# Scaled keys turned on VectorE in place of TensorE from chunk 12 on, in a fused linear-attention and maximum-of-three MLP kernel

## The chip, the cores and the metric

The kernel runs on one core of a Trainium2 chip. The metric is the device time of one execution in microseconds (us); less is better. A core has the engines TensorE (PE in the rows; PEld is its weight load), VectorE (DVE), ScalarE (ACT), GpSimd (POOL) and SyncE (SP), each with a queue of its own that it works through in order, and 16 DMA engines.

## The reference

A recurrent attention over 4 batches, 8 heads, 768 steps and 48 channels per head, and then an MLP whose hidden layer is the maximum of three products:

```python
for t in range(S):
    kt, vt, rt, wt = (k[:, :, t], v[:, :, t], r[:, :, t], w[:, :, t])
    cur = np.einsum('bhd,bhe->bhde', u[None] * kt, vt)
    y[:, :, t] = np.einsum('bhd,bhde->bhe', rt, state + cur)
    state = wt[:, :, :, None] * state + np.einsum('bhd,bhe->bhde', kt, vt)
...
h = np.maximum(np.maximum(x @ w1, x @ w2), x @ w3)
return (h @ w_out).astype(np.float32)
```

Here x is y laid out as 3072 tokens of 384 channels; the hidden layer has 768 channels. All inputs are float32.

## The kernel before

The sequence is cut into 6 chunks of 128 steps for each of the 4 batches, which makes 24 chunks k = 0 to 23 (the batch is k modulo 4, the place in the sequence k divided by 4). The attention of four chunks yields 512 tokens, a *half* in the program's words, and the MLP works on one half at a time: 18 groups of matmuls *up* (3 matrices x 6 blocks of the hidden layer; line 167), then 72 matmuls *down* (4 blocks of tokens x 6 blocks of the hidden layer x 3 terms; line 201). Apart from a part of the first half, each product is made of terms with a high and a low part of the operands (x_hi, x_lo, h_hi, h_lo), made by `split` (line 132 on ScalarE, line 133 on VectorE). `take_up` empties the PSUM tile of an up group: ScalarE copies the first of three (line 150), VectorE takes the maximum with the second and third (line 152).

A chunk of attention is a set of steps, each of one letter. Those that matter here:

- `b`, `p`, `q`, `f`, `r` (prep_scan_b to prep_rk): VectorE makes running products of the decay w forwards and backwards (scans at lines 399 and 414) and scales r and k in place in the loaded tile `tin` (line 423). The scaled keys, `kp`, lie with the channel in the partition: 112 partitions (two heads of 48, at 0 and at 64, with a gap of 16), 4 pairs of heads, 128 steps.
- `T` (transposes, line 492): turns `kp` so that the step lies in the partition: `kn`, 128 partitions, 4 pairs, 112 channels. TensorE does it by four transposes against `ident` (line 497) into a PSUM tile of the pool ps_m (four buffers, shared with the up and down groups and with `pu`), and ScalarE copies it out (line 499). Chunks 0 to 19 have this step; the last four pass no state on.
- `U` (to_state, line 518): TensorE multiplies `kn` with the values v into `pu`, the chunk's addition to the state; `S` (line 529) adds it on VectorE; `Z` (line 533) applies the decay.
- `X` (scores, line 477), `M` (take: a masked copy on VectorE, line 483, and a copy on ScalarE, line 486), `R` (from_state, line 508), `V` and `Y` (values, values_more, line 547): these make the chunk's output y in PSUM. Between V and Y stands a ScalarE copy of four columns of y, `touch` (line 553); Y's first matmul waits for it. `E` (result, line 565) copies y to x.
- `n` loads the next `tin` into one of three buffers, `tbuf[k % 3]`; `d`, `e` make the diagonal term, with GpSimd (lines 437, 438, 457).

The order of the work is written out by hand. Up to the end of the second half's MLP it is the string PARTS. After that six *units* for each k from 12 on are taken from the string ORD, and about one unit follows each MLP group; the number behind a letter is added to the chunk:

```python
ORD = "R0 V0 X1 Y0 U0 E0 b2 p2 d2 q2 | f2 n3 | S0 r2 Z2 c2 | e2 M1 | T1 | |"
```

So T for the next chunk comes in the fifth unit, and U uses its result in the first unit of the next round. Beside this runs `check_w` every third group: VectorE looks at a weight block (line 363), ScalarE squares and sums the result (line 365), and ScalarE's queue issues the load of the next block (line 368). ScalarE also empties the down groups (line 205), whose results SyncE's queue stores (line 688).

Of the kernel before, what the change touches and what calls it, by code (L numbers as in the profile page):

```python
# [29 lines left out]
F32 = mybir.dt.float32  # L30
# [11 lines left out]
B, H, S, D = 4, 8, 768, 48  # L42
DM, FF = 384, 768
NP = 4
C = 128
NCH = S // C
# [4 lines left out]
RK = -(-WU // 128) * 128  # L51
TU = RK + 2 * NP * C
# [40 lines left out]
PIECES = dict(a=(0, 1), b=(1, 2), c=(2, 4), d=(0, 2), e=(0, 4))  # L93
FIX = [*range(3 * FR, 3 * FT), *range(3 * FT + FR, NW), *range(3 * FR), *range(3 * FT, 3 * FT + FR)]
CS = 8
LATE = 2
LINE = 128
BIT = 16
# [4 lines left out]
def lines(n):  # L103

    return -(-n // LINE) * LINE
# [3 lines left out]
def kernel(ctx: ExitStack, tc, tin, nat, u_flat, u_pair, v_t, w_flat, out, ytr):  # L109
    nc = tc.nc  # L110
# [109 lines left out]
    with ExitStack() as fast:  # L220
# [6 lines left out]
        kn_p = pool("kn", 2)  # L227
# [9 lines left out]
        NB = 3  # L237
# [14 lines left out]
        def load(k):  # L252
            c, b = divmod(k, B)
            t = tbuf[k % NB]
            for cols in (slice(0, WU), slice(RK, TU)):
                if k == 0:
                    nc.sync.dma_start(out=t[0:64, cols], in_=tin[b, c, 0:64, cols])
                    nc.scalar.dma_start(out=t[64:112, cols], in_=tin[b, c, 64:112, cols])
                else:
                    nc.sync.dma_start(out=t[0:112, cols], in_=tin[b, c, :, cols])  # L260

        warm = cst.tile([128, 128], BF16, name="warm")
        nc.gpsimd.memset(warm[:, :], 0.0)
# [129 lines left out]
        prep = {}  # L393
# [23 lines left out]
        def prep_rk(k):  # L417

            t = tbuf[k % NB]
            both = t[:, RK:TU].rearrange("p (s a b) -> p s a b", s=2, a=NP)  # L420
            by = prep[k]["gf"][:, 0:2 * (WC + 2)].rearrange("p (s n) -> p s n", s=2)[:, :, 0:NP * WS]
            by = by.rearrange("p s (a b) -> p s a b", a=NP)[:, :, :, 0:C]
            nc.vector.tensor_tensor(out=both[0:112], in0=both[0:112], in1=by[0:112], op=ALU.mult)  # L423
            prep[k].update(rp=both[:, 0], kp=both[:, 1])

        def prep_check(k):
            flat = prep[k]["gf"][0:112, 0:2 * WC]
# [64 lines left out]
        def transposes(k):  # L492
            if goes_on(k):
                p = prep[k]
                pt = ps_m.tile([128, HT], F32, name="psm")
                for pr in range(NP):
                    nc.tensor.transpose(pt[:, pr * 112:pr * 112 + 112], p["kp"][0:112, pr, :], ident[0:112, 0:112])  # L497
                p["kn"] = kn = kn_p.tile([128, lines(NP * 112)], F32, name="kn")[:, 0:NP * 112].rearrange("p (a b) -> p a b", a=NP)
                nc.scalar.copy(out=kn[:, :, :].rearrange("p a b -> p (a b)"), in_=pt[:, 0:NP * 112])

        def from_state(k):
            p = prep.setdefault(k, {})
# [55 lines left out]
        def result(k):  # L558
# [11 lines left out]
            for lo in (0, 64) if due else ():  # L570
                for j in range(KT):
# [4 lines left out]
                     b=prep_scan_b, p=prep_floor, q=prep_inv, f=prep_scan_f, r=prep_rk, c=prep_check, d=prep_diag1, e=prep_diag2)  # L576
# [170 lines left out]
    with tc.If(rv != 0), ExitStack() as slow:  # L747
# [9 lines left out]
        with tc.For_i(0, B) as b:  # L757
            for pr in range(NP):
# [8 lines left out]
                for hh in range(2):  # L767
                    rows = slice(64 * hh, 64 * hh + 48)
# [90 lines left out]
def _layout(r, k, v, w, u, moe_w1, moe_w2, moe_w3, moe_w_out):  # L859

    def heads(a):
        return a.reshape(B, NP, 2, NCH, C, D).transpose(0, 3, 2, 5, 1, 4)

    tin = np.zeros((B, NCH, 112, TU), np.float32)
    tin[:, :, 48:64, :WC] = 1.0
    tin[:, :, :, :WC:WS] = 0.0
    for half in range(2):
        rows = tin[:, :, 64 * half:64 * half + D]
        rows[..., :NP * WS].reshape(B, NCH, D, NP, WS)[..., 1:] = heads(w)[:, :, half]
        rows[..., RK:RK + NP * C] = heads(r)[:, :, half].reshape(B, NCH, D, NP * C)  # L870
        rows[..., RK + NP * C:TU] = heads(k)[:, :, half].reshape(B, NCH, D, NP * C)
        rows[..., WC + half:WU:2] = u.reshape(NP, 2, D)[:, half].T

    def natural(a):
        return a.reshape(B, H, NCH, C, D).transpose(0, 2, 3, 1, 4).reshape(B, NCH, C, H * D)

    nv, turned = natural(v), lambda a: np.roll(a[..., H * D // 2:], HC, axis=2)
    parts = [nv, turned(nv)]
    for a in (natural(k), natural(r)):
        a = np.concatenate([a[..., 0:H * D // 2], turned(a)], axis=3)  # L880
        parts.append(a.reshape(B, NCH, C, NP, 2, D).swapaxes(3, 4).reshape(B, NCH, C, H * D))
    nat = np.concatenate(parts, axis=3)
    row = np.empty((KT, 128), np.int64)
    head = lambda j, par: 4 * (j % 2) + 2 * par + j // 2
    for j in range(KT):
        for par in range(2):
            row[j, 64 * par:64 * par + 48] = head(j, par) * D + np.arange(48)
            row[j, 64 * par + 48:64 * par + 64] = head(KT, par) * D + 16 * j + np.arange(16)
    ws = np.stack([moe_w1, moe_w2, moe_w3])
    w_in = ws[:, row.reshape(-1), :].reshape(3, KT, 128, FT, 128).transpose(3, 0, 2, 1, 4).reshape(3 * FT, 128, PC)  # L890
    w_all = np.concatenate([w_in, moe_w_out.reshape(FT, 128, DM)])
    if w_all.dtype == np.float64:
        w_all = np.append(w_all.reshape(-1), np.zeros(1)).view(np.int64)
    return {
        "tin": tin, "nat": nat, "u_flat": u.reshape(NP, 2, D).swapaxes(0, 1).reshape(H * D), "u_pair": u.reshape(NP, 2, D, 1),
        "v_t": v.transpose(0, 1, 3, 2), "w_all": w_all,
    }
# [18 lines left out]
```

## Time and profile before

| | |
|---|---|
| median of 3 runs | 414.88 us (414.78 to 415.26) |
| the profiled execution's own time | 414.63 us |
| its span, first to last instruction | 412.2 us |
| PE busy | 398.8 us (97%) |
| DVE busy | 266.1 us (65%) |
| ACT busy | 175.0 us (42%) |
| POOL busy | 83.9 us (20%) |
| granted TensorE clock, mean | 0.998 |

All times in rows are counted from the start of the span. The busy time of an engine counts each moment once, while the durations of its instructions overlap: the next one starts before the last has ended. The distance from start to start therefore tells more of a price than the duration. In the rows an operation is written as tile written <- tiles read, with partitions x elements; "x4" at the end of a row of the timeline says that four instructions are merged in it. What stands in brackets is the idle time of the engine just before, and what ended it.

### The profile page before, as it was taken

Reading aid. Unit: us, or ns where it says so; the run is one execution under the profiler, and the core shown is the slowest. Engines: PE = TensorE matmul, PEld = TensorE weight load, DVE = VectorE, ACT = ScalarE, POOL = GpSimd, SP = SyncE. Lnnn points to the kernel's source line nnn. Section 1 sums busy time; section 2 is a strip of 40 time slices with the busy share of each in tenths; the row PEclk is TensorE's granted clock in tenths of the full one; section 3 lists DMA queues with packets and bytes.
Section 4 is the critical chain, followed back from the end, with each engine's and each line's share of the span. In section 5 each row is a group of like instructions: output and inputs, shape, how many; then the busy total and the mean of one; then the engine's idle time right before and its main releaser. Section 6 shows DMA issues by size and latency. Waiting matters only on the chain.

```text
span 412.2 us, 9386 instructions
## 1 busy us (share of the span) xinstructions
PE 398.8 (97%) x3852; PEld 328.9 (80%) x3852; DVE 266.1 (65%) x446; ACT 175.0 (42%) x401; POOL 83.9 (20%) x92
## 2 busy tenths in 40 slices
PE   8898999899999999999999999999999999999994
PEld 3566877687788888988889988888978888988894
DVE  6998999997859777447568467658558623233320
ACT  1466667654543253514524534434534432411210
POOL 4240142404026141123303113203113100000000
PEclk9999999999999999999999999999999999999999
DMA  8948895902442150482643582533592121200001
GB/s 215 326 153 257 266 289 197 271 3 55 151 153 78 53 180 14 132 264 61 195 142 119 157 297 74 175 112 131 152 310 83 38 78 59 78 1 2 2 21 64
DMA packets 23844, 55.69 MB, mean 135 GB/s; under 512 B 3280, under 2 KB 6672, under 8 KB 23792
## 3 DMA queue, kind: packets, MB, share of 16 engines
q1 hardware_dynamic: 20160, 45.56, 36.1%
q10 hardware_dynamic: 3632, 9.44, 7.2%
q8 instruction: 32, 0.52, 0.5%
q14 instruction: 20, 0.16, 0.1%
HBM read 49.10 MB, written 4.72 MB: 131 GB/s over the span
## 4 chain that ended last, share of the span: by engine, by line
PE 83%; DVE 8%; DMA 3%; issue 2%; ACT 1%; SPq 1%; DVEq 0%; ACTq 0%
PE psm L167 53%; PE psm L201 15%; PE y L547 3%; DMA tin<-in_tin_dram 3%; PE grams L477 3%; PE y L508 3%; PE psm L518 2%; DVE gf L414 2%; PE grams L201 2%; PE psm L497 1%; DVE gf L399 1%; DVE tin L423 1%; DVE kr L434 1%; DVE w L342 1%; SPq L573 1%
## 5 line engine op out<-in xcount | busy, mean ns | idle before, releaser
L167 PE MATMUL psm<-x_hi,w 128*128 128x512 f32 x576 | 185.3, 395 | 0.0
L167 PEld LDWEIGHTS psm<-x_hi,w 128*128 128x128 f32 x576 | 108.1, 188 | 23.1 <-issue 0.2
L167 PE MATMUL psm<-x_lo,w 128*128 128x512 f32 x288 | 112.2, 390 | 0.0
L152 DVE TENSOR_TENSOR m<-psm,m 128x512 f32<-128x512 f32 x64 | 44.0, 688 | 70.3 <-PE psm L167 65.4
L457 POOL TENSOR_SCALAR_AFFINE_SELECT a<-sums 64x512 f32<-64x512 f32 x48 | 44.1, 919 | 207.2 <-DVE sums L453 117.6
L201 PE MATMUL psm<-w,h_hi 128*128 128x384 f32 x264 | 70.1, 362 | 0.0
L167 PEld LDWEIGHTS psm<-x_lo,w 128*128 128x128 f32 x288 | 54.1, 188 | 10.6
L201 PEld LDWEIGHTS psm<-w,h_hi 128*128 128x128 f32 x264 | 47.7, 188 | 4.9
L132 ACT CAST h_hi<-m 128x512 fp32r<-128x512 f32 x32 | 19.7, 620 | 52.2 <-DVE m L152 52.2
L201 PE MATMUL psm<-w,h_lo 128*128 128x384 f32 x116 | 38.9, 335 | 0.0
L399 DVE TENSOR_TENSOR_SCAN gf<-tin,d_bwd 112x517 f32<-112x517 f32 x24 | 32.8, 1366 | 6.1 <-DMA tin<-in_tin_dram 6.1
L167 PE MATMUL psm<-x,w 128*128 128x256 f32 (+1 forms) x126 | 33.7, 416 | 1.6 <-DVE w L342 1.0
L133 DVE TENSOR_TENSOR h_lo<-m,h_hi 128x512 fp32r<-128x512 f32 x32 | 22.4, 704 | 16.9 <-ACT h_hi L132 16.7
L414 DVE TENSOR_TENSOR_SCAN gf<-tin,d_fwd 112x517 f32<-112x517 f32 x24 | 31.1, 1296 | 0.2
L167 PEld LDWEIGHTS psm<-x,w 128*128 128x128 f32 x126 | 23.0, 190 | 9.1 <-issue 3.5
L428 ACT ACTIVATE gf<-gf 112x1034 f32<-112x1034 f32 x24 | 25.7, 1071 | 10.3 <-DVE tin L423 10.3
L423 DVE TENSOR_TENSOR tin<-tin,gf 112x1024 f32<-112x1024 f32 x24 | 30.0, 1252 | 0.1
L547 PE MATMUL y<-a,v 64*64 64x128 f32 (+3 forms) x768 | 25.7, 247 | 3.4 <-ACT touch L553 3.0
L547 PEld LDWEIGHTS y<-a,v 64*64 64x64 f32 (+1 forms) x768 | 21.9, 126 | 8.1 <-ACT touch L553 4.0
L150 ACT COPY m<-psm 128x512 f32<-128x512 f32 x32 | 18.6, 582 | 16.2 <-PE psm L167 15.4
L437 POOL TENSOR_TENSOR kr<-kr 128x384 f32<-128x384 f32 x16 | 17.2, 1077 | 33.9 <-DMA kr<-in_nat_dram 32.9
L133 DVE TENSOR_TENSOR x_lo<-x,x_hi 128x512 fp32r<-128x512 f32 x18 | 13.2, 781 | 16.8 <-ACT x_hi L132 13.0
(75 smaller groups left out, 447.7 us busy)
## 6 DMA issues: line engine op xcount, KB each, us to landing
tin<-in_tin_dram SPq DMA_DIRECT2D x23, 448.0 KB, 4.4
w<-in_w_all_dram SPq DMA_DIRECT2D x25, 384.0 KB, 8.3
w<-in_w_all_dram ACTq DMA_DIRECT2D x23, 384.0 KB, 3.2
v<-in_nat_dram SPq DMA_DIRECT2D x24, 288.0 KB, 5.8
kr<-in_nat_dram SPq DMA_DIRECT2D x16, 384.0 KB, 5.3
tin<-in_tin_dram SPq DMA_DIRECT2D x23, 229.7 KB, 6.1
out_dram<-m SPq DMA_DIRECT2D x22, 192.0 KB, 2.1
x<-x SPq DMA_DIRECT2D x30, 32.0 KB, 2.0
```

What stands on the lines that cost most here:

```text
L132: nc.scalar.copy(out=hi, in_=src)
L133: rest = lambda: nc.vector.tensor_tensor(out=lo, in0=src, in1=hi.bitcast(F32), op=ALU.subtract)
L150: nc.scalar.copy(out=m[:, cols], in_=ps[:, cols])
L152: nc.vector.tensor_tensor(out=m[:, cols], in0=ps[:, cols], in1=m[:, cols], op=ALU.max)
L167: nc.tensor.matmul(ps[:, cols], lhsT=wt[i][:, ct * 128:(ct + 1) * 128], rhs=x[part][:, ct, cols], start=(n == 0), stop=(n == KT * len(term ...
L201: nc.tensor.matmul(pss[tt][:, 0:DM], lhsT=ht[f][:, tok], rhs=wt[FT * 3 + f][:, :], start=(f == 0 and i == 0), stop=(f == FT - 1 and i == l ...
L399: nc.vector.tensor_tensor_scan(out=g[0:112, ::-1], data0=t[0:112, 0:WC][:, ::-1], data1=d_bwd[0:112, ::-1], initial=0.0, op0=ALU.mult, op1 ...
L414: nc.vector.tensor_tensor_scan(out=prep[k]["f"][0:112, :], data0=tbuf[k % NB][0:112, 0:WC], data1=d_fwd[0:112, :], initial=0.0, op0=ALU.mu ...
L423: nc.vector.tensor_tensor(out=both[0:112], in0=both[0:112], in1=by[0:112], op=ALU.mult)
L428: nc.scalar.activation(out=flat, in_=flat, func=AF.Square, accum_out=acc[0:112, k:k + 1])
L457: nc.gpsimd.affine_select(out=a[o:o + HC, 0:H, :], in_=cs[o:o + HC, :].unsqueeze(2).broadcast_to([HC, H, HC]), pattern=[[0, H], [1, HC]], ...
L547: nc.tensor.matmul(y[o:o + m, hh, s, HC:C] if part else y[o:o + m, hh, s, :], lhsT=natt[k][0][q:q + 64, at:at + m], rhs=p["a"][q:q + 64, o ...
```

## The change

For chunks 12 to 19 the step T issues sixteen VectorE instructions and nothing on TensorE or ScalarE. Each turns blocks of 32 partitions x 32 columns, one for each of the four pairs, and puts them to the mirrored place: source partitions j to j+31 and columns i to i+31 go to partitions i to i+31, columns j to j+31. j changes with every instruction, i after four. Since blocks of 32 rows cover 128 partitions, rows 112 to 127 are read as well; the array in memory is therefore given 128 rows, of which the last 16 are zero, and the loads of chunks 9, 10 and 11 bring all 128 rows into the three buffers. Nothing writes these rows afterwards. The tile `kn` holds 128 columns a pair in place of 112 for all chunks, so the ScalarE copy of chunks 0 to 11 writes four separate runs of 112.

```diff
+TK = 12
...
-                    nc.sync.dma_start(out=t[0:112, cols], in_=tin[b, c, :, cols])
+                    rows = slice(0, 128 if TK - NB <= k < TK else 112)
+                    nc.sync.dma_start(out=t[rows, cols], in_=tin[b, c, rows, cols])
...
-            prep[k].update(rp=both[:, 0], kp=both[:, 1])
+            prep[k].update(rp=both[:, 0], kp=both[:, 1], kp128=t[:, RK + NP * C:TU].rearrange("p (a b) -> p a b", a=NP))
...
         def transposes(k):
             if goes_on(k):
                 p = prep[k]
+                p["kn"] = kn = kn_p.tile([128, NP, C], F32, name="kn")
+                if k >= TK:
+                    for i in range(0, C, 32):
+                        for j in range(0, C, 32):
+                            nc.vector.transpose(out=kn[i:i + 32, :, j:j + 32], in_=p["kp128"][j:j + 32, :, i:i + 32])
+                    return
                 pt = ps_m.tile([128, HT], F32, name="psm")
                 for pr in range(NP):
                     nc.tensor.transpose(pt[:, pr * 112:pr * 112 + 112], p["kp"][0:112, pr, :], ident[0:112, 0:112])
-                p["kn"] = kn = kn_p.tile([128, lines(NP * 112)], F32, name="kn")[:, 0:NP * 112].rearrange("p (a b) -> p a b", a=NP)
-                nc.scalar.copy(out=kn[:, :, :].rearrange("p a b -> p (a b)"), in_=pt[:, 0:NP * 112])
+                nc.scalar.copy(out=kn[:, :, 0:112], in_=pt[:, 0:NP * 112].rearrange("p (a b) -> p a b", a=NP))
...
-    tin = np.zeros((B, NCH, 112, TU), np.float32)
+    tin = np.zeros((B, NCH, 128, TU), np.float32)
```

The other instructions keep their order on every engine. Line numbers of the changed kernel are higher by 1 (from line 95 on), 2 (from 261 on) and 7 (behind the transposes). Where the instructions go is shown at the two places with the largest terms of the prediction.

VectorE around the transposes of chunk 15 and of chunk 16, in the changed kernel (L365 is the weight check, before L363; L134 the low parts, L401 the backward scan):

```order
L153 TENSOR_TENSOR m<-psm,m 128x512
L134 TENSOR_TENSOR h_lo<-m,h_hi 128x512
L501 STREAM_TRANSPOSE kn<-tin_107 32x4x32 x16
L365 TENSOR_SCALAR cv<-w_2252 128x384
L401 SCALAR_TENSOR_TENSOR gf<-tin_109,d_bwd 112x517
...
L485 COPY_PREDICATED a<-mask,grams 128x512
L134 TENSOR_TENSOR x_lo<-x,x_hi 128x512 x3
L501 STREAM_TRANSPOSE kn<-tin_108 32x4x32 x16
L365 TENSOR_SCALAR cv<-w_2252 128x384
L401 SCALAR_TENSOR_TENSOR gf<-tin_107,d_bwd 112x517
```

Before, the weight check followed on h_lo and on x_lo directly; now sixteen transposes stand between.

ScalarE at the same place of chunk 15, from the cast h_hi to touch, before:

```order
L132 CAST h_hi<-m 128x512
L499 COPY kn<-psm 128x448
L365 ACTIVATE cv,sums<-cv,mid_top 128x384
L368 DMA w_2242<-in_w_all_dram 128x384
L205 COPY m<-psm 128x384
L553 COPY touch<-y 112x4
```

and now (L367 is the squaring of the weight check, L206 the emptying of a down group, L560 touch):

```order
L133 CAST h_hi<-m 128x512
L367 ACTIVATE cv,sums<-cv,mid_top 128x384
L370 DMA w_2252<-in_w_all_dram 128x384
L206 COPY m<-psm 128x384
L560 COPY touch<-y 112x4
```

The copy of kn is gone; the rest stands in the order of before, with the squaring, which reads what the weight check on VectorE wrote, ahead of touch. On TensorE the row `L497 MATMUL psm<-ident,tin_108 128x112 x4` and its like are taken out eight times, and nothing else moves.

## Rows read from the trace of the kernel before

**Rows 1.** Busy time by stretch: length, then busy us and count of each engine, clock, DMA.

```profile
160.00:300.00 140.00, 140.00 (x1407) 122.91 (x1400) 86.75 (x142) 60.27 (x141) 29.47 (x34) 1.00 0.49 152
```

**Rows 2.** The chain of waits in order of time: start, length, what.

```profile
189.60 0.39 PE psm L497 x4
```

**Rows 3.** Timeline of PE around the transposes of chunks 13 and 15: start, length.

```profile
188.29 0.39 PE L167 MATMUL psm<-x_lo,w 128*128 128x512 f32 x1
...
188.97 0.39 PE L167 MATMUL psm<-x_lo,w 128*128 128x512 f32 x1
...
190.07 0.39 PE L167 MATMUL psm<-x_lo,w 128*128 128x512 f32 x1
...
221.24 0.34 PE L201 MATMUL psm<-w,h_lo 128*128 128x384 f32 x1
...
221.77 0.34 PE L201 MATMUL psm<-w,h_lo 128*128 128x384 f32 x1
...
222.70 0.34 PE L201 MATMUL psm<-w,h_lo 128*128 128x384 f32 x1
```

**Rows 4.** Groups of ACT, 165 to 300 us: count, busy us, mean ns, idle before.

```profile
L499 ACT COPY kn<-psm 128x448 f32<-128x448 f32 x8 | 4.3, 534 | 7.0 <-PE psm L497 7.0
```

**Rows 5.** DMA issues: count, KB each, median us to landing.

```profile
tin<-in_tin_dram SPq DMA_DIRECT2D x23, 448.0 KB, 4.4
```

**Rows 6.** Short VectorE instructions: timeline at 357 us, and a group of 165 to 300.

```profile
357.12 0.18 DVE L653 TENSOR_REDUCE good<-sums 112x1 f32<-112x24 f32 x1
357.22 0.17 DVE L656 TENSOR_SCALAR sums<-sums 128x24 f32<-128x24 f32 x1
357.42 0.18 DVE L657 TENSOR_REDUCE good<-sums 128x1 f32<-128x24 f32 x1
...
L529 DVE TENSOR_TENSOR scur<-psm,sstar 112x192 f32<-112x192 f32 x8 | 2.8, 352 | 2.9 <-PE psm L518 2.9
```

**Rows 7.** Timeline of PE at the second value products of chunk 20.

```profile
304.78 0.56 PE L547 MATMUL y<-a,v 64*64 64x128 f32 x16 [0.77 <-ACT touch L553]
```

**Rows 8.** Timelines of DVE, ACT and PE behind the transposes of chunk 15.

```profile
222.84 1.17 DVE L363 TENSOR_SCALAR cv<-w 128x384 uint32<-128x384 uint32 x1
...
224.05 0.62 ACT L365 ACTIVATE cv<-cv,mid_top 128x384 f32<-128x384 uint32 x1 [0.98 <-DVE cv L363]
...
224.66 0.46 ACT L205 COPY m<-psm 128x384 f32<-128x384 f32 x1
226.64 0.16 ACT L553 COPY touch<-y 112x4 f32<-112x4 f32 x1 [1.52 <-PE y L547]
...
227.06 0.52 PE L547 MATMUL y<-a,v 64*48 64x128 f32 x16
```

**Rows 9.** Timelines of DVE, ACT and PE behind the transposes of chunk 16.

```profile
237.02 0.36 DVE L363 TENSOR_SCALAR cv<-w 128x384 uint32<-128x384 uint32 x1
...
238.79 0.59 ACT L150 COPY m<-psm 128x512 f32<-128x512 f32 x1 [0.67 <-ACT cv L365]
...
242.16 0.52 PE L547 MATMUL y<-a,v 64*48 64x128 f32 x16
```

**Rows 10.** Timelines of DVE, ACT and PE behind the transposes of chunk 13.

```profile
189.63 0.69 DVE L152 TENSOR_TENSOR m<-psm,m 128x512 f32<-128x512 f32 x1 [1.09 <-PE psm L167]
...
190.45 0.62 ACT L132 CAST h_hi<-m 128x512 fp32r<-128x512 f32 x1
...
195.54 0.52 PE L547 MATMUL y<-a,v 64*48 64x128 f32 x16
```

**Rows 11.** Timelines of DVE and PE at the transposes of chunk 14.

```profile
203.77 0.37 DVE L363 TENSOR_SCALAR cv<-w 128x384 uint32<-128x384 uint32 x1 [0.72 <-DMA w<-in_w_all_dram]
...
205.10 0.69 DVE L152 TENSOR_TENSOR m<-psm,m 128x512 f32<-128x512 f32 x1 [0.37 <-PE psm L167]
...
213.04 0.52 PE L547 MATMUL y<-a,v 64*48 64x128 f32 x16
```

## The prediction, made before the changed kernel had run

> **What bounds the kernel now.** I read the busy shares by stretch first, then the chain of waits, then the timelines of the four engines around each place where the four transposes stand. In the stretch that holds all eight affected chunks TensorE is busy for 140.00 of 140 us at the full granted clock, VectorE for 86.75 and ScalarE for 60.27 [rows 1]. So every us that leaves TensorE's queue there is a us of the kernel, unless something makes TensorE wait. The chain agrees: each group of transposes is a link of its own on it [rows 2]. VectorE has 53 us free in the stretch. Its share is not the question. What is: where the sixteen transposes stand in its queue, and what stands behind them.
>
> **What leaves TensorE.** The spacing of matmuls gives the price better than the durations, which overlap. In the up phase the distance between two x_lo matmuls, three matmuls, is 188.97 - 188.29 = 0.68 us, and 190.07 - 188.97 = 1.10 us where the transposes stand between: 0.42 us for the four. In the down phase it is 221.77 - 221.24 = 0.53 and 222.70 - 221.77 = 0.93: 0.40 us [rows 3]. Of the eight chunks (12 to 19) four have them in the up phase (13, 14, 17, 18) and four in the down phase (12, 15, 16, 19): 4 x 0.42 + 4 x 0.40 = **3.3 us gained**. The eight ScalarE copies of 534 ns [rows 4] lie beside TensorE's work, which never waited for them in the stretch; they count as nothing, but their places in ScalarE's queue become free. The copies of chunks 0 to 11 now write four runs of 112 words in place of one of 448: same elements, off the path, nothing. The loads of chunks 9 to 11 carry 128 rows for 112; the larger piece takes 4.4 us [rows 5], so a seventh more is 0.6 us on loads that are issued chunks ahead: nothing.
>
> **What a transpose costs on VectorE.** No row shows one. It has 4 x 32 = 128 elements a partition. A line through short and middle VectorE rows (24 elements 0.18 us, 192 elements 352 ns) has a slope of about one element a ns and a base of about 0.155 us: some **0.29 us** of duration for 128. What counts is from start to start, p. Two ends [rows 6]: the reduction at 357.12 took 0.18 us, yet the next instruction, which doesn't need it, starts at 357.22, 0.08 before its end; so overlapped p = 0.21. The instruction at 357.42 needs its predecessor (357.22, 0.17 us): 0.20 from start to start, 0.03 or 0.04 over the duration; so at most p = 0.33. The sixteen don't need each other, which speaks for 0.21. But the overlap in the rows is between instructions that all begin at partition 0, in and out, and here each of the sixteen reads another block of 32 partitions than the one before it. No row shows an overlap across such a change, and a transposed row can't be written before its block is read. So I don't count on it: p from 0.29 to 0.33, taken at the middle, **0.31**: sixteen make a burst of 16 x 0.31 = **4.96 us**, eight bursts 40 us, which fit into VectorE's 53 free us in sum, though not everywhere in place.
>
> The Trainium skill, VectorE: DVE Perf Modes, section "Two Vector instructions with no wait between them", states that an instruction whose first input or output starts in another quadrant of 32 partitions than the last one's is held until all earlier Vector instructions have finished. By that rule none of the sixteen overlaps; by the rows' overlap all do, and the sum below would be 1.9 us faster in place of 2.5 us slower. No trace so far holds such a pair. The same page ("The three transpose paths") gives 311 ns for a VectorE transpose of 128x128 bf16; taken as p, an estimate, it would give the same sum.
>
> **Where a burst falls.** TensorE does not wait for kn itself: it is used a unit or more later. It waits for touch (L553): its second half of the value products may not start before that ScalarE copy, and ScalarE works in order. The trace of before has this wait already, 0.77 us at 304.78 [rows 7]. So for each burst I follow what VectorE hands to ScalarE ahead of the next touch, and compare with TensorE's arrival, which is now 0.40 or 0.42 us earlier.
>
> - **Chunk 15.** The burst takes the place at 222.84, and L363 (the weight check) waits behind it until 222.84 + 4.96 = 227.80; it takes 0.36 us undisturbed (its 1.17 here is the exception). ScalarE's L365 needs it, and L205 and touch stand behind L365: 0.61 us from L365's start to L205's, 0.46 for L205, 0.16 for touch [rows 8]. That is 227.80 + 0.36 + 0.61 + 0.46 + 0.16 = 229.39. TensorE arrives at 227.06 - 0.40 = 226.66. It waits **2.7 us**.
> - **Chunk 16.** The burst starts at 237.02; behind it L363, then on ScalarE L365, L150 (0.59 us), touch: 237.02 + 4.96 + 0.36 + 0.61 + 0.59 + 0.16 = 243.70 against 242.16 - 0.40 = 241.76 [rows 9]: **1.9 us**.
> - **Chunk 13.** VectorE is free at 189.63 - 1.09 = 188.54. Behind the burst the maximum L152 (0.69), then L132 (0.62), L150 (0.59), touch (0.16): 195.56 against 195.54 - 0.42 = 195.12 [rows 10]; less some 0.1 of overlap, **0.3 us**. Chunk 17 has the same order and the same distances: **0.3**.
> - **Chunk 14.** Free at 205.10 - 0.37 = 204.73; behind the burst L152, L132, the subtraction L133 (about as long as L152), L363, L365, touch: 204.73 + 4.96 + 0.69 + 0.62 + 0.69 + 0.36 + 0.61 + 0.16 = 212.82 against 213.04 - 0.42 = 212.62 [rows 11], 0.2 us. But the L363 ahead of this burst waited 0.72 us for a weight load, which is issued only when the check before it is through, and that one now stands behind chunk 13's burst. Up to 0.9 in all; I take **0.6**.
> - **Chunks 12, 18, 19.** Nothing on which a near touch depends stands behind the burst closely: chunk 18 has one more group of matmuls before its touch, 12 and 19 have neither a check nor a maximum between. Nothing.
>
> PSUM is not short: of the four psm buffers the transposes no longer take one, and a maximum that is 4 to 5 us late leaves the next three groups their buffers.
>
> Sum: 2.7 + 1.9 + 0.6 + 0.3 + 0.3 = 5.8 us lost, 3.3 gained: **+2.5 us**. The profiled execution took 414.63 us; 417.1. The median of the runs, 414.88, is 0.25 above it: **417.4 us**. With p = 0.29 the waits are 2.4 + 1.6 + 0.3 = 4.3 and the sum is +1.0 (415.9); with p = 0.33 they are 3.0 + 2.2 + 0.9 + 0.6 + 0.6 = 7.3 and it is +4.0 (418.9).
>
> **Rivals.** *The transposes overlap.* p = 0.21, burst 3.4 us: chunk 15 then waits 1.1, chunk 16 0.3, the others nothing: 1.4 lost, 3.3 gained, 413.0 us. For it speaks that the sixteen are independent and that rows of independent neighbours overlap; against it that no row overlaps across blocks of partitions. It decides from p = 0.265 downwards, where chunk 15 and 16 together lose what TensorE gains.
>
> *Two elements a step.* L363, one input from SBUF, does 384 elements in 0.36 us, nearly twice the rate of the others [rows 9]. If a transpose could do so, p would be about 0.14 to 0.22, the bursts 2.3 to 3.5 us, and nearly the whole gain would stay: 411.6 to 413. Against it: it is no plain elementwise operation.
>
> *A transpose that takes two steps an element*, for 4-byte data: 0.155 + 0.27 = 0.42 us, burst 6.7. Each of the five waits grows by about 1.8 us, some 9 more in all: 426. Nothing in the rows asks for it.
>
> *TensorE was waiting anyway*, so that its 3.3 us are not on the path, and the bursts find slack: no change. The 140.00 of 140 us speak against it.
>
> **How the numbers follow.** The forecast (no overlap, p 0.29 to 0.33) gets 0.60, of which 0.04 falls so low that it can't be told from no change; the overlap 0.25, of which 0.02 likewise; the double rate 0.05; the half rate 0.06; no change 0.04. About 0.2% (0.8 us) is what a measurement of this kernel can tell from none. So slower 0.62, no change 0.10, faster 0.28. The range from 412.5 to 420.5 holds the first two cases with the bounds of p; it leaves out the half rate, most of the double rate, and a forecast with waits that I have missed. Since both signs have weight, the forecast's own range is 415.7 to 419.2.
>
> **What would show it.** In the changed profile: transposes of about 0.29 us that start 0.29 to 0.33 apart (0.21 would make the rival right); TensorE's spacing without the 1.10 and 0.93; TensorE idle before the second value products of chunks 15 and 16, released by touch, 2 to 3 and about 2 us, and little elsewhere; ScalarE's L365 waiting for L363 by some 4 us more at both. Wrong would be a TensorE that waits for kn or for a psm buffer instead, or no new idle time on it at all.

## The result, and the profile after

The changed kernel took **420.26 us** (median of four runs, 418.84 to 422.85) against 415.07 us before on the same chip: a ratio of 1.0127, 95% interval 1.0104 to 1.015. It is slower by 5.2 us, where the prediction had 2.5. The four runs took 418.84, 419.63, 420.89 and 422.85 us at a mean granted clock of 0.993, 0.990, 0.989 and 0.985: the lower the clock, the longer. The profiled one is the shortest, 418.84 us with a span of 417.1.

The stretch of [rows 1], from the busy times by stretch:

```profile
160.00:300.00 140.00, 135.21 (x1374) 118.23 (x1367) 119.46 (x267) 52.98 (x126) 29.52 (x33) 0.99 0.47 143
```

TensorE is no longer busy throughout: 135.21 us in place of 140.00. VectorE went from 86.75 to 119.46, ScalarE from 60.27 to 52.98, and the clock has left 1.00. The shares of the chain of waits, from the page, where before they were 83% for PE and 8% for DVE (VectorE's transposes, L501, alone have 6% now; TensorE's of [rows 2], L497, had 1% in all):

```profile
PE 67%; DVE 20%; ACT 4%; issue 4%; DMA 2%; ACTq 1%; SPq 0%; DVEq 0%
```

The price of a transpose, from the groups (count, busy us, mean ns, idle before) and the timeline of VectorE in chunk 15, is to be compared with [rows 6]:

```profile
L501 DVE STREAM_TRANSPOSE kn<-tin 32x128 f32<-32x128 f32 x128 | 38.7, 302 | 1.7
...
222.43 5.07 DVE L501 STREAM_TRANSPOSE kn<-tin 32x128 f32<-32x128 f32 x16
227.52 0.36 DVE L365 TENSOR_SCALAR cv<-w 128x384 uint32<-128x384 uint32 x1
```

One takes 0.302 us, and sixteen take 5.07, so (5.07 - 0.30) / 15 = 0.32 us from start to start. Next come ScalarE behind the bursts of chunks 15 and 16, with the burst of 16 (to be compared with [rows 8, 9]), and all idle times of TensorE over 0.2 us from chunk 13 on, except one of 0.34 us in chunk 23, which the kernel before has too. The row of 225.55 has no wait and stands there for its distance to the next (timelines; in brackets the idle time before an instruction and what ended it):

```profile
227.92 0.61 ACT L367 ACTIVATE cv<-cv,mid_top 128x384 f32<-128x384 uint32 x1 [6.44 <-DVE cv L365]
...
228.53 0.46 ACT L206 COPY m<-psm 128x384 f32<-128x384 f32 x1
228.89 0.16 ACT L560 COPY touch<-y 112x4 f32<-112x4 f32 x1
...
239.85 5.06 DVE L501 STREAM_TRANSPOSE kn<-tin 32x128 f32<-32x128 f32 x16
...
245.34 0.61 ACT L367 ACTIVATE cv<-cv,mid_top 128x384 f32<-128x384 uint32 x1 [5.00 <-DVE cv L365]
...
246.42 0.16 ACT L560 COPY touch<-y 112x4 f32<-112x4 f32 x1
...
195.54 0.56 PE L554 MATMUL y<-a,v 64*64 64x128 f32 x16 [0.24 <-ACT touch L560]
...
225.55 0.86 PE L479 MATMUL grams<-tin 48*64 48x64 f32 x32
229.11 0.56 PE L554 MATMUL y<-a,v 64*64 64x128 f32 x16 [2.70 <-ACT touch L560]
...
246.63 0.56 PE L554 MATMUL y<-a,v 64*64 64x128 f32 x16 [1.09 <-ACT touch L560]
...
262.15 0.56 PE L554 MATMUL y<-a,v 64*64 64x128 f32 x16 [0.28 <-ACT touch L560]
...
294.17 0.56 PE L525 MATMUL psm<-v,kn 128*48 128x48 f32 x14 [0.34 <-DVE kn L501]
...
309.31 0.56 PE L554 MATMUL y<-a,v 64*64 64x128 f32 x16 [0.84 <-ACT touch L560]
```

The chain that was forecast stands in them link by link: the burst ends at 227.50, the check on VectorE follows, then the check on ScalarE, a copy, touch, and TensorE starts at 229.11 after 2.70 us of nothing. The last of these waits (309.31) is that of [rows 7], 0.77 before.

The idle time in brackets is not all that a wait costs. Matmuls overlap in the rows, and a wait takes this overlap away too. Before, the second value products of chunk 15 started 227.06 - 226.39 = 0.67 us after the scores (grams), although these last 0.86:

```profile
226.39 0.86 PE L477 MATMUL grams<-tin 48*64 48x64 f32 x32
```

Now they start 229.11 - 225.55 = 3.56 us after them, which is 2.89 us later, 0.19 more than the idle 2.70. In the same way (scores at 194.45, 244.68 and 261.01) chunk 13 is 0.41 us late, chunk 16 1.28 and chunk 17 0.47. In chunk 19 the distance from the second value products to the first matmul of the MLP behind the state products went from 1.05 to 1.80 us, 0.75 more: the trace has 0.34 us of it as the idle time above and 0.14 as one too short for the list.

What was not forecast comes right behind chunk 15's wait. The busy times by stretch, and TensorE's timeline:

```profile
230.00:232.00 2.00, 2.00 (x15) 1.92 (x11) 2.00 (x3) 0.42 (x2) 0.00 (x0) 0.52 0.54 187
232.00:234.00 2.00, 2.00 (x9) 2.00 (x8) 1.74 (x5) 0.44 (x2) 0.68 (x2) 0.62 0.15 33
234.00:236.00 2.00, 2.00 (x13) 2.00 (x12) 0.00 (x0) 1.69 (x5) 0.63 (x1) 1.00 0.56 142
...
231.02 0.52 PE L202 MATMUL psm<-w,h_lo 128*128 128x384 f32 x1
...
231.98 0.52 PE L202 MATMUL psm<-w,h_lo 128*128 128x384 f32 x1
...
234.27 0.34 PE L202 MATMUL psm<-w,h_lo 128*128 128x384 f32 x1
...
234.80 0.33 PE L202 MATMUL psm<-w,h_lo 128*128 128x384 f32 x1
```

TensorE is busy all the time here, yet three matmuls take 231.98 - 231.02 = 0.96 us in place of 234.80 - 234.27 = 0.53. The granted clock reads 0.52 and 0.62: for most of these 4 us it is the lower of its two levels, 1.2 GHz in place of 2.4. Before, every stretch here reads 1.00.

Where the time went, chunk by chunk. The state matmuls that open a chunk (L508 before, L515 after) start at these times:

| opens chunk | before | after | difference | step | in the step |
|---|---|---|---|---|---|
| 5 | 64.58 | 65.00 | +0.42 | | not the change (see run 8) |
| 12 | 178.59 | 178.62 | +0.03 | -0.39 | chunk 12's transposes gone |
| 13 | 194.05 | 193.63 | -0.42 | -0.45 | chunk 13's gone |
| 14 | 211.56 | 211.13 | -0.43 | -0.01 | chunk 14's gone, wait of 0.24 |
| 15 | 225.57 | 224.74 | -0.83 | -0.40 | chunk 15's gone |
| 16 | 240.68 | 243.87 | +3.19 | +4.02 | chunk 16's gone, wait of 2.70, half clock |
| 17 | 256.14 | 260.19 | +4.05 | +0.86 | chunk 17's gone, wait of 1.09 |
| 18 | 273.65 | 277.76 | +4.11 | +0.06 | chunk 18's gone, wait of 0.28 |
| 19 | 287.67 | 291.36 | +3.69 | -0.42 | chunk 19's gone |
| 20 | 302.35 | 306.80 | +4.45 | +0.76 | wait for kn of 0.34 |

Steps without a wait gain 0.39 to 0.45 us each, as forecast. Chunk 15 alone costs 4.02 + 0.40 = 4.4 us: 2.9 of lateness and 1.5 of half clock. The steps from chunk 5 to chunk 20 sum to 4.45 - 0.42 = 4.0 us.

The whole execution is 418.84 - 414.63 = 4.2 us longer, but its span is 417.1 - 412.2 = 4.9 us longer: some 0.7 us is saved ahead of the first or behind the last instruction, where no row tells of it. Every execution on record shows this: kernels with no chunk or one chunk on VectorE spend 2.1 to 2.6 us outside the span, those with six or eight 1.7 to 1.9. No run tells why.

### The profile page after: what moved, and what is told of

The parts are those of the page before. It is cut to its first block, busy times and chain, and to the rows that moved or that the text cites. A ratio compares the mean times of both kernels' runs of the same rounds, so it can differ in the third digit from the quotient of the medians.

```text
span 417.1 us, 9443 instructions
## 1 busy us (share of the span) xinstructions
PE 398.6 (96%) x3820; PEld 327.8 (79%) x3820; DVE 300.5 (72%) x574; ACT 170.7 (41%) x393; POOL 82.0 (20%) x92
## 4 chain that ended last, share of the span: by engine, by line
PE 67%; DVE 20%; ACT 4%; issue 4%; DMA 2%; ACTq 1%; SPq 0%; DVEq 0%
PE psm L168 45%; PE psm L202 13%; DVE kn L501 6%; PE y L554 3%; DVE gf L416 2%; DVE gf L401 2%; PE psm L525 2%; PE y L515 2%; DVE tin L425 2%; PE grams L479 2%; PE grams L202 2%; DMA tin<-in_tin_dram 1%; DVE w L344 1%; DVE cv L333 1%; DVE a L485 1%
## 5 line engine op out<-in xcount | busy, mean ns | idle before, releaser
L459 POOL TENSOR_SCALAR_AFFINE_SELECT a<-sums 64x512 f32<-64x512 f32 x48 | 42.4, 883 | 221.6 <-DVE sums L455 149.2
L202 PEld LDWEIGHTS psm<-w,h_hi 128*128 128x128 f32 x264 | 48.9, 192 | 4.9
L501 DVE STREAM_TRANSPOSE kn<-tin 32x128 f32<-32x128 f32 x128 | 38.7, 302 | 1.7
L401 DVE TENSOR_TENSOR_SCAN gf<-tin,d_bwd 112x517 f32<-112x517 f32 x24 | 31.2, 1299 | 1.9 <-DMA tin<-in_tin_dram 1.9
L134 DVE TENSOR_TENSOR h_lo<-m,h_hi 128x512 fp32r<-128x512 f32 x32 | 22.4, 702 | 12.6 <-ACT h_hi L133 12.5
L367 ACT ACTIVATE cv<-cv,mid_top 128x384 f32<-128x384 uint32 x24 | 14.8, 615 | 34.7 <-DVE cv L365 34.7
L134 DVE TENSOR_TENSOR x_lo<-x,x_hi 128x512 fp32r<-128x512 f32 x18 | 13.1, 779 | 15.3 <-ACT x_hi L133 15.3
```

Source lines behind the costliest of these rows:

```text
L134: rest = lambda: nc.vector.tensor_tensor(out=lo, in0=src, in1=hi.bitcast(F32), op=ALU.subtract)
L202: nc.tensor.matmul(pss[tt][:, 0:DM], lhsT=ht[f][:, tok], rhs=wt[FT * 3 + f][:, :], start=(f == 0 and i == 0), stop=(f == FT - 1 and i == l ...
L401: nc.vector.tensor_tensor_scan(out=g[0:112, ::-1], data0=t[0:112, 0:WC][:, ::-1], data1=d_bwd[0:112, ::-1], initial=0.0, op0=ALU.mult, op1 ...
L459: nc.gpsimd.affine_select(out=a[o:o + HC, 0:H, :], in_=cs[o:o + HC, :].unsqueeze(2).broadcast_to([HC, H, HC]), pattern=[[0, H], [1, HC]], ...
L501: nc.vector.transpose(out=kn[i:i + 32, :, j:j + 32], in_=p["kp128"][j:j + 32, :, i:i + 32])
```

## The experiments

The theory after the result: the burst delays the weight check, the check delays touch, TensorE waits, and a long wait also halves TensorE's clock for some us. Of the code only the lines that decide are shown. Line numbers in the experiments are up to 13 higher than above, and each edit is against the changed kernel unless it says otherwise. All ratios are to the kernel before.

**1. Chunks 15 and 16 back to TensorE.**

```diff
+BACK = (15, 16)
-                if k >= TK:
+                if k >= TK and k not in BACK:
```

> Chunks 15 and 16 go back to TensorE's transposes and ScalarE's copy; 12, 13, 14, 17, 18, 19 stay on VectorE. Theory (a burst ahead of the weight check holds up touch, and the long wait at chunk 15 then halves TensorE's clock for a while): gain 2 x 0.40 + 4 x 0.42 = 2.5 us, small waits that the changed kernel shows at 13, 17 and 19 of 0.4, 0.5 and 0.8, so about 0.8 us faster than before (414.3), no wait of over 0.5 us before the second value products of 15 and 16, no stretch at half clock between 220 and 250 us. Rival (VectorE is simply too full): 30 of the 39 us of transposes are still there, so still 3 to 4 us slower than before.

Measured: 414.0 us (413.01 to 416.52), ratio 0.9978, interval 0.9963 to 0.9994. From chunk 12 to 19 TensorE waits 0.23, 0.28 and 0.34 us (chunks 13, 17, 19), and no stretch is at half clock; the wait of chunk 20, 0.77 before, is 1.10 here. So the other six chunks are a small gain, some half of it outside the span (the median span is 412.2 us against 412.7), and the loss belongs to these two.

**2. Only chunk 15 on VectorE** (`BACK = (12, 13, 14, 16, 17, 18, 19)`).

> Only chunk 15 is turned on VectorE, all others on TensorE as before. Theory: the wait of 2.7 to 2.9 us at its touch comes back alone, and the half clock after it: 2.8 + 1.5 to 4 - 0.4, so 4 to 6 us slower than before (419 to 421) with a mean clock under 0.995. Rival (VectorE too full): one burst of 5 us in 53 free ones costs nothing, 0.4 us faster. Second rival (the half clock comes from the missing transposes, not from the wait): the wait is there, the clock stays full, 2.4 us slower.

Measured: 419.34 us (418.55 to 421.12), ratio 1.0107, interval 1.008 to 1.0134. The wait is again 2.70 us, and the clock of 228 to 232 and of 232 to 236 us is 0.78 and 0.79. One chunk's sixteen transposes cost 419.34 - 415.14 = 4.2 us.

**3. The check issued ahead of the units of its group.**

```diff
+            if groups % 3 == 0:
+                check_w()
             while units < min(UPH + groups * UPH // GPH, UNITS):
                 unit()
                 take_x()
-            if groups % 3 == 0:
-                check_w()
```

> All eight chunks on VectorE as in the change, but every weight check of the regular part is issued ahead of the unit of attention of its group in place of behind it, so that VectorE has the check's instruction ahead of the transposes of 15 and 16. Theory: no wait for touch of over 0.5 us at 15 and 16, no half clock; 3.3 gained, some 2 us left in small waits (kn itself at 15 and 19 among them): 0.5 to 1.5 us faster than before (413.6 to 414.6). Rival (VectorE too full): as slow as the change, 418 to 422.

Measured: 426.14 us, ratio 1.0255, interval 1.0227 to 1.0282: a miss. The burst that delays the check in chunk 15 comes from a unit of an earlier group, so moving the check within its own group does not bring it past the burst; it only puts the check ahead of touch in more chunks. TensorE's waits for touch, from its timeline (chunks 13, 15, 16, 17, 18, 19), and the stretches below full clock:

```profile
196.54 0.56 PE L554 MATMUL y<-a,v 64*64 64x128 f32 x16 [1.33 <-ACT touch L560]
...
230.11 0.91 PE L554 MATMUL y<-a,v 64*64 64x128 f32 x16 [2.70 <-ACT touch L560]
...
247.99 0.56 PE L554 MATMUL y<-a,v 64*64 64x128 f32 x16 [1.59 <-ACT touch L560]
...
264.88 0.56 PE L554 MATMUL y<-a,v 64*64 64x128 f32 x16 [1.69 <-ACT touch L560]
...
282.42 0.56 PE L554 MATMUL y<-a,v 64*64 64x128 f32 x16 [0.27 <-ACT touch L560]
...
298.79 0.91 PE L554 MATMUL y<-a,v 64*64 64x128 f32 x16 [2.57 <-ACT touch L560]
...
228.00:232.00 4.00, 1.89 (x33) 1.68 (x33) 3.58 (x7) 1.82 (x6) 0.00 (x0) 0.75 0.45 145
...
300.00:304.00 4.00, 4.00 (x24) 3.91 (x22) 3.90 (x7) 0.47 (x3) 0.58 (x1) 0.50 0.31 96
```

It still tells something: in this run the clock fell after the waits of 2.70 and 2.57 us and not after those of 1.33, 1.59 and 1.69.

**4. The price of a transpose by itself.** Sixteen more ahead of the right ones, which overwrite them: in chunk 12 with the same partitions in and out, in chunk 13 the input's block of 32 partitions changes each time, in chunk 14 the output's; in chunk 18 eight over all 128 partitions.

```diff
+BLOCKS = [(i, j) for i in range(0, 128, 32) for j in range(0, 128, 32)]
+TRY = {12: [(0, 0, j, i) for i, j in BLOCKS], 13: [(0, j, j, i) for i, j in BLOCKS], 14: [(j, 0, i, j) for i, j in BLOCKS]}
+                    for o, a, j, i in TRY.get(k, ()):
+                        nc.vector.transpose(out=kn[o:o + 32, :, j:j + 32], in_=p["kp128"][a:a + 32, :, i:i + 32])
```

> Sixteen extra transposes ahead of the right ones, whose result is overwritten, in chunks 12 (always partitions 0 to 31 in and out), 13 (in changes, out stays at 0), 14 (in stays at 0, out changes), and eight in chunk 18 over all 128 partitions (four of 4 x 32, four of 4 x 128). If the change of partition blocks is what forbids the overlap: 0.21 us from start to start in the first four of chunk 12 (the later ones also wait for one another's output), 0.30 to 0.32 in 13 and 14. If a transpose never overlaps: 0.30 to 0.32 everywhere. 128 partitions: the same 0.30 for 4 x 32; 0.69 for 4 x 128 at one element a step, 0.42 at two.

Measured, in VectorE's timeline and groups (441.12 us in all, one run):

```profile
168.34 3.19 DVE L502 STREAM_TRANSPOSE kn<-tin 32x128 f32<-32x128 f32 x16
...
188.12 5.26 DVE L502 STREAM_TRANSPOSE kn<-tin 32x128 f32<-32x128 f32 x16
...
211.23 5.13 DVE L502 STREAM_TRANSPOSE kn<-tin 32x128 f32<-32x128 f32 x16
...
L504 DVE STREAM_TRANSPOSE kn<-tin 128x512 f32<-128x512 f32 x4 | 2.8, 711 | 0.1
```

On the same partitions they overlap: 0.20 us each. Where the input's or the output's block changes they do not: 0.33 and 0.32. The 512 elements of the larger form in 0.711 us exclude both the double and the half rate of the rivals.

This run's bursts are longer than the change's, and its trace also shows a long wait without half clock, before chunk 18's second value products:

```profile
278.65 0.56 PE L560 MATMUL y<-a,v 64*64 64x128 f32 x16 [2.11 <-ACT touch L566]
...
280.00:282.00 2.00, 2.00 (x10) 1.61 (x10) 1.97 (x4) 0.15 (x1) 0.00 (x0) 1.00 1.02 388
```

The ten us behind it all read 1.00.

**5. TensorE kept busy in chunk 15's wait.** As run 2, with matmuls on zeros into a buffer that nothing reads; they take 2.76 us where TensorE stood idle for 2.70.

```diff
+            if k == 15:
+                warmer(12)
```

> As the run with chunk 15 alone on VectorE, and twelve matmuls of 128x512 bf16 on zeros into a PSUM tile that nothing reads are put on TensorE where it waits for chunk 15's touch (such matmuls took 0.21 us each start to start at the start of the program, so some 2.6 us of the 2.7). Mine (a long idle time of TensorE lowers its clock afterwards): the touch comes at the same time, TensorE is not idle over 0.5 us there, the granted clock stays 1.00 after it, and the 1.6 us of half clock go: 417.2 to 417.9 us, where chunk 15 alone took 419.34. Rival (the clock falls for another reason, the idle time of the engine has no part in it): half clock after it all the same, 419 to 420 us.

Measured: 417.48 us (416.88 to 418.42), ratio 1.0069, interval 1.0049 to 1.0089: 2.6 us above the kernel before, where run 2 has 4.2. The stretches of run 2 and, below them, of this run (busy times, then the clock):

```profile
228.00:232.00 4.00, 2.06 (x33) 1.86 (x34) 3.75 (x8) 1.82 (x6) 0.00 (x0) 0.78 0.44 147
232.00:236.00 4.00, 4.00 (x20) 4.00 (x20) 2.80 (x6) 1.57 (x4) 1.31 (x2) 0.79 0.27 55
```

```profile
226.81 2.76 PE L598 MATMUL psm<-warm 128*128 128x512 bf16 x12
...
228.00:232.00 4.00, 4.00 (x48) 2.79 (x46) 3.90 (x7) 1.81 (x6) 0.00 (x0) 1.00 0.48 149
232.00:236.00 4.00, 4.00 (x25) 4.00 (x25) 2.23 (x5) 2.47 (x6) 1.31 (x2) 1.00 0.52 145
```

The useful work waits as long as before, the clock stays at 1.00, and the chunk is done 18.00 us after its start (225.21 to 243.21) in place of 19.47 (225.57 to 245.04). So the half clock follows from TensorE being idle there, and it costs 1.5 us.

**6. A shorter burst in chunk 15**, alone on VectorE as in run 2: one transpose over all partitions and twelve small ones; the last block row of kn is left out.

```diff
+                    nc.vector.transpose(out=kn[:, :, :], in_=p["kp128"][:, :, :])
-                    for i in range(0, C, 32):
+                    for i in range(0, 96, 32):
```

> As the run with chunk 15 alone on VectorE, with one transpose of 128x512 (0.71 us) and twelve of the sixteen small ones in place of all sixteen: the last block row of kn is left wrong. The burst is 0.71 + 12 x 0.316 = 4.5 us in place of 5.06, so the wait for the touch should be 2.70 - 0.56 = 2.1 us. Waits of 1.09 to 1.69 us brought no half clock in the runs so far, those of 2.57 and 2.70 did. If 2.1 us bring it too, 1.6 us of it: 418.3 to 419 us. If not: 415.1 + 2.1 - 0.4 = 416.8 us, 416.5 to 417.2, and granted clock 1.00 after it. I hold the second a little likelier.

Measured: 419.06 us, ratio 1.0106, interval 1.009 to 1.0123. The wait is 2.16 us, as worked out, but the half clock came (0.83 and 0.74 in the two stretches), so the likelier of the two expectations missed. The chunk takes 244.31 - 225.29 = 19.02 us, against 19.47 in run 2.

**7. Only chunk 16 on VectorE** (`BACK = (12, 13, 14, 15, 17, 18, 19)`).

> Only chunk 16's transposes on VectorE. In the changed kernel chunk 16 waited 1.09 us for its touch where the prediction had 1.9; there chunk 15's wait and half clock came just ahead of it. Theory 1 (the 1.9 was right for chunk 16 by itself, and TensorE, made late by chunk 15, met a burst that was less late): a wait of 1.6 to 1.9 us here; with the full clock after it 415.0 + 1.75 - 0.4 = 416.3 us, with half clock for 1.5 us some 418. Theory 2 (the chain behind chunk 16's burst was put together wrongly): 1.0 to 1.2 us here too, no half clock, and 415.7 us. I hold the first likelier. [...]

Measured: 418.49 us (416.88 to 420.25), ratio 1.007, interval 1.0045 to 1.0094. In the profiled run:

```profile
237.26 5.06 DVE L502 STREAM_TRANSPOSE kn<-tin 32x128 f32<-32x128 f32 x16
242.36 1.05 DVE L366 TENSOR_SCALAR cv<-w 128x384 uint32<-128x384 uint32 x1
...
244.73 0.91 PE L555 MATMUL y<-a,v 64*64 64x128 f32 x16 [2.61 <-ACT touch L561]
...
246.00:248.00 2.00, 2.00 (x16) 1.66 (x13) 0.73 (x1) 0.40 (x2) 0.00 (x0) 0.50 0.83 287
248.00:250.00 2.00, 2.00 (x6) 1.58 (x5) 0.00 (x0) 0.00 (x0) 0.00 (x0) 0.50 0.72 248
```

The wait is longer than either expectation, because the check took 1.05 us here in place of 0.36 ([rows 8] had one of 1.17); without that 0.69 it is 1.9, the forecast's value. So the forecast's chain for chunk 16 holds where chunk 15 does not come ahead of it, as far as one trace and this subtraction show. One of the four executions, 416.88 us, has a mean granted clock of 1.00: the wait was shorter in it or brought no half clock, and its trace is not kept.

Beside the long check GpSimd was at work:

```profile
242.19 0.99 POOL L441 TENSOR_TENSOR kr<-kr,u_bc 128x384 f32<-128x384 f32 x1
```

The check starts while this product runs (242.36) and ends 0.23 us after it (243.41 against 243.18); the last section has more of these.

**8. All transposes back on TensorE**, with the wider kn, its copies and the wider loads kept (`BACK = range(24)`).

> All transposes go back to TensorE; what stays of the change is the wider kn (128 columns a pair, of which the ScalarE copy writes 112) and the loads of 128 rows where they were. It tests the 0.42 us by which the changed kernel is late before its first VectorE transpose (chunk 9's state matmuls at 65.0 in place of 64.58). If the layout or the loads cost this, 415.3 to 415.6 us and the first start of the state matmuls at 65.0; if it is the difference of two executions, 414.9 to 415.2 us and 64.6. No wait for the touch that the kernel before does not have, in both.

Measured: 415.06 us, ratio 1.0004, interval 0.9995 to 1.0012: the layout costs nothing. The state matmuls meant here open chunk 5, not 9. They start at 65.03 us in this run, but at 64.50 in run 1 and 65.01 in run 2, which have the same program up to there, so the 0.42 us is a difference of executions, and nothing of the change.

**9. Quarters.** The sixteen in four groups of four, at four places of the order of steps.

```diff
-ORD = "R0 V0 X1 Y0 U0 E0 b2 p2 d2 q2 | f2 n3 | S0 r2 Z2 c2 | e2 M1 | T1 | |"
+ORD = "R0 V0 X1 Y0 U0 E0 b2 p2 d2 q2 | f2 n3 t1 | S0 r2 Z2 c2 t1 | e2 M1 t1 | t1 | T1 |"
...
+                for q in range(turned.get(k, 0), min(turned.get(k, 0) + n, 4)):
+                    i = 32 * q
+                    for j in range(0, C, 32):
+                        nc.vector.transpose(out=kn[i:i + 32, :, j:j + 32], in_=p["kp128"][j:j + 32, :, i:i + 32])
...
+                    elif step[0] == "t":
+                        quarter(k + int(step[1]))
```

> The sixteen transposes of a chunk are cut into four groups of four (one block row of kn each), put at four places of the order of steps, so that a check or a split on VectorE has at most 4 x 0.316 = 1.27 us of them ahead of it in place of 5.06. Mine (the burst is what TensorE waits for, through the check on ScalarE and the touch; the half clock follows only from the long wait): no wait for the touch over 0.3 us in chunks 12 to 19 that the kernel before does not have, granted clock 1.00 in every stretch of 4 us from 160 to 300, and the eight chunks' transposes saved: 8 x 0.41 = 3.3 us, less some small waits and the 0.4 us that the changed kernel loses ahead of chunk 12; 411.5 to 413 us. Rival 1 (VectorE's added 40 us of work as such, not the length of the burst, make TensorE late): the waits come back spread over the chunks, 416 to 420. Rival 2 (the half clock has to do with the mix of work, not with the wait): stretches at half clock here too, each at 1.5 us or more.

Measured: 418.73 us, ratio 1.0092, interval 1.0078 to 1.0106: a miss of 6 us. Touch comes in time in chunks 12 to 19 but for 0.32 us in chunk 14, but TensorE waits elsewhere (its timeline, ahead of chunks 15 and 19):

```profile
225.29 0.62 PE L202 MATMUL psm<-w,h_hi 128*128 128x384 f32 x2 [2.01 <-ACT h_hi L133]
...
290.08 0.62 PE L202 MATMUL psm<-w,h_hi 128*128 128x384 f32 x2 [2.03 <-ACT h_hi L133]
```

Half clock follows both (0.88 from 224 to 228 us and 0.69 from 228 to 232 us, 0.59 from 292 to 296 us). VectorE shows why TensorE waits, for the first: quarters stand ahead of the last maximum of the up-projection, and the split that TensorE reads next waits for it.

```profile
219.22 1.25 DVE L505 STREAM_TRANSPOSE kn<-tin 32x128 f32<-32x128 f32 x4
...
222.61 1.26 DVE L505 STREAM_TRANSPOSE kn<-tin 32x128 f32<-32x128 f32 x4
223.90 0.69 DVE L153 TENSOR_TENSOR m<-psm,m 128x512 f32<-128x512 f32 x1
225.27 0.89 DVE L134 TENSOR_TENSOR h_lo<-m,h_hi 128x512 fp32r<-128x512 f32 x1 [0.68 <-ACT h_hi L133]
```

**10. Quarters one to two groups earlier** (`E0 t1 b2 p2 d2 q2 t1 | f2 n3 t1 | S0 r2 Z2 c2 t1 |`).

> All eight chunks in quarters, as in the run with quarters, but each chunk's quarters one to two groups earlier in the order of steps, so that none is left to stand between the last maxima and the last split before a down-projection. VectorE was idle for 6.3 us of 206 to 221 us where TensorE does all transposes, and a chunk's burst takes 5.06 of it. If that room is enough: no wait over 0.5 us and 411.5 to 413 us. If VectorE reaches the last maxima late all the same: waits of 0.5 to 1.5 us for the cast of the split before chunks 15 and 19, 413 to 416 us. I hold the second likelier, as the room is short.

Measured: 420.2 us in six of seven executions (418.98 to 422.10), ratio 1.0123, interval 1.0104 to 1.0143: worse than both expectations. The profile is of the seventh, 427.78 us at a clock of 0.978, and its later rows compare with nothing. Its first wait, still at full clock until then, is 1.70 us for the same cast before chunk 15 and 0.69 more for the split: the second expectation's place, with more than its price.

**11. Quarters, with chunks 15 and 19 on TensorE** (run 9 and `BACK = (15, 19)`).

> As the run with quarters, but chunks 15 and 19 go back to TensorE: their quarters stood between the last maxima and the last split of an up-projection on VectorE, and TensorE, which turns to the down-projection there and reads that split first, waited 2.01 and 2.03 us for it, with half clock after each. Mine: both waits and both stretches of half clock go, and six chunks save 0.41 us each, less the 0.32 us for a touch in chunk 14: 415.0 - 2.5 + 0.3 = 412.8 us, 412.3 to 413.5, faster than the kernel before. Rival (what VectorE has to do in all makes TensorE late somewhere, wherever the pieces stand): waits at other places, 414 to 417 us.

Measured: **412.74 us** (412.06 to 412.75) against 414.93, ratio 0.994, interval 0.9927 to 0.9952: faster than both kernels. Of the 2.2 us, 1.8 are in the span (410.9 against 412.7 in the median); the rest lies outside it, as in all kernels with six or eight chunks on VectorE, and the expectation of 412.8 did not have it. TensorE has one new wait, and the clock is 1.00:

```profile
212.95 0.56 PE L567 MATMUL y<-a,v 64*64 64x128 f32 x16 [0.33 <-ACT touch L573]
...
160.00:296.00 136.00, 135.67 (x1393) 119.25 (x1393) 115.19 (x238) 56.27 (x132) 30.37 (x34) 1.00 0.50 150
```

VectorE is busy for 115 of 136 us here (85%, as in the changed kernel's 119 of 140), so its load as such makes nobody late; where the pieces stand does.

## Why the prediction was right and wrong

**The gain**, 3.3 us: right. The steps without a wait show 0.39 to 0.45 us a chunk against 0.40 and 0.42.

**The price of a transpose**: right. p = 0.32 against 0.31, the burst 5.07 against 4.96. The choice between 0.21 and 0.31 was made by the change of partitions from one transpose to the next, and run 4 shows that this decides: 0.20 on the same partitions, 0.33 and 0.32 across blocks. The rule of the Trainium skill, VectorE: DVE Perf Modes, section "Two Vector instructions with no wait between them", that an instruction whose input or output starts in another block of 32 partitions than the last one's is held until the earlier ones have finished, agrees with these rows, for the input and for the output.

**The waits for touch**: the mechanism right, the sizes mixed, the sum right by luck. The prediction compared starts with starts, so its waits answer to the lateness above and not to the idle times. Chunk 15: 2.7 forecast, 2.89 measured. Chunk 13: 0.3, 0.41. Chunk 17: 0.3, 0.47. Chunk 16: 1.9, 1.28. TensorE, just made late by chunk 15, opened chunk 16 4.02 us after the burst began (239.85 and 243.87), where the forecast had 3.26 (237.02 in [rows 9], and 240.68 - 0.40); in run 7, with nothing ahead, it is 3.19 (237.26 and 240.45), and the 1.9 is there. Chunk 14: 0.6, none; the check ahead of its burst did not wait for its weights, and the burst started at 204.07 in place of 204.73. "TensorE does not wait for kn itself" was right for seven chunks and wrong for chunk 19, which is 0.75 us late: the burst from 289.05 to 294.11 ends after the products' turn. With that one the sum is 0.41 + 2.89 + 1.28 + 0.47 + 0.75 = 5.8 us, the 5.8 of the forecast, but only because chunk 19's part, which it did not have, and what 13, 15 and 17 have too much make up for what 14 and 16 have too little.

**The step that failed** is the sum itself, "2.7 + 1.9 + 0.6 + 0.3 + 0.3 = 5.8 us lost": it ends a wait's price where TensorE starts again, and has no term for the speed at which it goes on. The prediction reads the full granted clock in the trace of before and takes it to stay. After the 2.70 us of idle time TensorE's matmuls ran at half clock, which cost 1.5 us (run 5: 19.47 - 18.00; chunk 15's step: 4.4 - 2.9). With that term the stretch from chunk 5 to chunk 20 is accounted for: 5.8 late, 1.5 of half clock, 3.3 gained, +4.0, where the table has 4.45 - 0.42 = 4.0.

The rest is not the forecast's chain. Of the profiled run's +4.2, 0.4 had come before chunk 5, without the change (run 8); 0.4 more of span came behind chunk 20's start, 0.1 of it by chunk 20's wait (0.84 for 0.77) and the rest unexplained; and 0.7 was saved outside the span. From the profiled run to the median there are 420.26 - 418.84 = 1.4 us more. An estimate by the mean clock, (0.993 - 0.9895) x 417 = 1.5 us, would put them down to more half clock, but no trace of those executions is kept, and the estimate does not hold everywhere: two of run 3's, at 0.995 and 0.981, are 2.2 us apart, where it gives 5.9.

**The rivals**: overlap fell by the price, both other rates by run 4, and "waiting anyway" by the steps of -0.4. The direction held, and the range to 420.5 by 0.2 us; the forecast's own range, 415.7 to 419.2, did not.

## What to carry to other kernels

Work that is moved to an engine with room is priced by what stands behind it in that engine's queue, and followed through every engine that works in order behind it, up to the one that sets the time. A wait of the bounding engine can cost more than its length: ask how long a single wait gets, not only what they sum to, since the half clock behind one of 2.70 us cost 1.5 us more here, and behind one of 2.61 us 2.9. Pieces of a quarter of the burst, kept away from the two chunks where VectorE's last maximum is what TensorE turns to next, made of +5.2 us a gain of 2.2 (run 11).

## What the runs showed of the hardware that was not expected

TensorE's clock fell to its lower level after idle times of 2.01 (with 0.31 more behind it) and 2.03 us (run 9), 2.16 (run 6), 2.57 (run 3), 2.61 (run 7) and 2.70 us (the changed kernel, runs 2 and 3), and after four of 2.60 to 5.53 us in run 4. After those of 1.09 to 1.69 us it did not (the changed kernel, runs 1, 3, 4 and 9), and neither after one of 2.11 us in run 4. So it does not go by the length of the idle time alone; what else decides, no run tells. How long the clock stayed down varies more than the wait: some 3.5 us of time after 2.70 in the changed kernel, some 6 after 2.61 in run 7. There chunk 16 takes 261.61 - 240.45 = 21.16 us in place of 256.14 - 240.68 = 15.46, and with 2.8 us for the wait and its lost overlap the half clock costs 2.9 us. Matmuls on zeros in the idle time kept the clock up (run 5).

The same VectorE check of 128x384 takes 0.33 to 0.49 us in most places and up to 1.18 in some. In twelve traces (all but run 10's) each check of 0.64 us or more starts while GpSimd multiplies (the line of kr and u_bc, or that of kr alone) and ends 0.2 us after that product: before, 222.84 to 224.01 us, with the product from 222.45 to 223.80. No run moved the product, so the cause is not shown.

The time saved outside the span, some 0.7 us with six or eight chunks on VectorE, is told with the result; its cause is open.
